# A linear recurrence and a bilinear feed-forward on one core: block 0's up products alone during the weight conversion, and part of block 1 in triples

## The chip, the cores and the metric

One NeuronCore of a Trainium2 chip runs the whole program. The time is device microseconds (us) from the first to the last instruction of an execution, with what lies around them. The kernel before took 598.5 us as the median of three runs (598.17 to 599.41).

The core has five engines that work side by side, each on its own queue in order: PE (matrix products), DVE (element-wise and scans), ACT (activation functions and copies), POOL (element-wise, slower) and SP, which here only issues transfers. An instruction that waits holds everything behind it on its own engine.

## The reference

Two layers in sequence. Layer 1 is a recurrence for each of 4 x 8 heads with a 48 x 48 state; layer 2 is a bilinear feed-forward on 3072 tokens of 384 channels:

```python
f = 1 / (1 + exp(-f_logit))
for t in range(768):
    state = f[:, :, t, :, None] * state + einsum('bhd,bhe->bhde', k[:, :, t], v[:, :, t])
    y[:, :, t] = einsum('bhd,bhde->bhe', q[:, :, t], state)
x = y.transpose(0, 2, 1, 3).reshape(3072, 384)
out = ((x @ w_a) * (x @ w_b)) @ w_out      # w_a, w_b: 384 x 1536, w_out: 1536 x 384
```

`q, k, v, f_logit` arrive as 32-bit floats, the three weight matrices as 64-bit floats.

## The kernel before, in words

**Attention units and blocks.** The 3072 tokens form 8 blocks of 384 (`BLK`). The recurrence of a block is done in two units (four heads each), 16 units in all. Unit 2b and 2b+1 make block b. A unit's *front* (`front_parts`) is: two sigmoids on ACT (one of 1-f with its accumulator), one affine step on POOL, and on DVE scans and the products into `k_in` and `q_in`. Its *core* (`core_parts`) is small matmuls on PE (scores L387, transposes L411, gains L435, within L484, across L510) with a mask on DVE, a copy of the transposes on ACT (`turned`, L420), state additions on DVE, copies out on ACT and stores to `xT`, which is the block's x with channels on the partitions. Scores need `q_in` of their unit.

**The feed-forward of a block.** The d_ff axis has 12 tiles (`ft`) of 128. An *up* (`up_steps`, L593) is one `ft` of one block done directly: three matmuls 128x128 by 128x384 into the bank of b, then three into the bank of a. Each 32-bit matmul of the program is two hardware matmuls in the trace, so an up is 12 of them. Then `product` copies b out of its bank on ACT (the *factor copy*, L613) and multiplies a by it on DVE (L615). There are four banks `ps_f`, handed out in turn, so that up n takes the banks of up n-2: its first half can begin only when the factor copy of up n-2 has been made, its second half only when the product of up n-2 has been taken.

Blocks 2 to 7 do not use ups. They use *triples* (`up_triples`, L715): for j = 0..3, three `ft` at once (j, j+4, j+8) by an algorithm with 15 block products of half width instead of 18. It needs sums of rows of x (`combine_x`, L699) and sums of columns of the weights (`combine_w_ba`), and costs copies on ACT (L1271) and additions on DVE (L707). Products with `w_out` (`down`, L808) take two groups of 128 tokens at a time, by seven products instead of eight, with sums of `w_out` (`combine_w_out`) and of the operands.

**Converting the weights.** The 64-bit weights arrive as 20 pieces (`weight_pieces`): b and a alternate, piece 0 and 1 for ft 0, 2 and 3 for ft 1-2, up to 10 and 11 for ft 9-10, the half-sized 12 and 13 for ft 11; 14 to 19 are `w_out`. The conversion of one (`from_double`) is: on ACT an `Abs` of the high words (L58), an `Identity` of the low words (L59), a `Sign` (L62) and a `Relu` of that (L63), on POOL a minimum (L60) behind the `Abs`, on DVE a shift (L68) behind POOL and an addition into the weights (the *put*, L73, in three rows for pieces 0 to 13). The intermediate buffers `thirds` and `bits` are three deep: the `Abs` of piece i overwrites what the put of piece i-3 reads. Raw pieces land in four places `raws4`; pieces 4 and 5 land in rows 0 and 1 of `groups`.

**The order.** Up to about 66 us of the span the order on every engine is written out by hand: units 0 to 3, pieces 0 to 9, and the ups of block 0 for ft 0 to 5. Then, before the change, the rest of the ups alternate between block 1 and block 0 (`ups`, L1087), so that the weights are needed at half the rate. The first 13 of these are in the written-out part, with conversions between them; the last 5 and all that follows (`main`) are given to a list scheduler. This planner walks through `main`, the sequence of PE products with the copies and sums that free their banks, and places the steps of side lines (`Line`: sums of `w_out`, sums of x, unit cores, unit fronts, loads, sums of `w_ba`) wherever by its own costs (`BEAT` 653 ns for a product of `main`, a load for each step) they delay no step of `main` beyond its due beat. It decides the order on each engine before the kernel runs; on the chip only semaphores hold. `past` and `needs` are a line's conditions, `marks`/`beside` force a line to be done ahead of a point of `main`.

Of the sums of `w_ba` before the change, two- and three-term sums are made by ACT copies (`write`, 6 of them, L628) and accumulating transfers on the POOL queue (`add_by_dma`, 11 of them, L625), and four by DVE additions (L1226).

Of the kernel before, what the change touches and what calls it, by code (L numbers as in the profile page):

```python
# [22 lines left out]
BLK = 384  # L23
# [113 lines left out]
def by_quotients(ctx, tc, q, k, f_logit, v, moe_w_a, moe_w_b, moe_w_out, out, ident, weights, bad):  # L137
# [53 lines left out]
    raw_places = itertools.cycle([raws4[:, PIECE * i:PIECE * i + PIECE] for i in range(4)])  # L191
# [43 lines left out]
    EARLY = (4, 5)  # L235
# [3 lines left out]
    def load_weights(n=1):  # L239
        for _ in range(n):  # L240
# [4 lines left out]
            if src.dtype != FP32:  # L245

                if len(raws) in EARLY:
                    raw = groups[:, EARLY.index(len(raws))].bitcast(mybir.dt.uint64)
                else:
                    raw = next(raw_places)  # L250
                raw = raw[:, 0:k * m].rearrange("p (k m) -> p k m", k=k)
# [18 lines left out]
    def end(n):  # L270

        while ended[0] < min(n, len(todo)):
            begin(ended[0] + 1)
            next(going[ended[0]], None)
            ended[0] += 1
            if ended[0] > 2 and ended[0] - 1 not in EARLY:
                load_weights()

    def convert(n):
        while ended[0] < min(n, len(todo)):  # L280
            end(ended[0] + 1)
            begin(ended[0] + 2)
# [6 lines left out]
    firsts = groups[:, len(EARLY)].rearrange("p (u n s) -> p u n s", u=NQ, n=2)  # L289
# [317 lines left out]
    def product():  # L607

        if not factors:
            return  # L610
        blk, ft, ps = factors.pop(0)
        b_sb = next(b_copies)
        nc.scalar.copy(b_sb, ps["b"][:, 0:BLK])  # L613
# [10 lines left out]
    def add_by_dma(to, x):  # L624
        nc.gpsimd.dma_start(out=to, in_=x, accum_op=ALU.add)  # L625

# [3 lines left out]
    def w_sums(steps, width):  # L630

        for to, x, what in steps:
            if what in (1, -1):
                yield ACT, width, 0, write, to, x, what
            elif what == "+":
                yield POOL, 1300, 0, add_by_dma, to, x
            else:
                yield DVE, width + 200, 0, nc.vector.tensor_tensor, to, x, *what
# [19 lines left out]
    def combine_w_ba():  # L658
# [10 lines left out]
        )  # L669
        return w_sums((  # L670
            (s[1], a12, 1), (s[4], a33, -1), (s[5], a11, -1), (s[1], a22, "+"), (s[4], a31, "+"), (s[5], a31, "+"),
            (s[3], a22, 1), (s[2], a12, 1), (s[0], a21, 1), (s[1], a23, "+"), (s[4], a21, "+"), (s[5], a32, "+"),
            (s[3], a23, "+"), (s[2], a22, "+"), (s[0], a32, "+"), (s[3], a32, "+"), (s[2], a21, "+"),
        ), 1000), w_sums((
            (a31, a11, (a31, ALU.subtract)), (a31, a31, (a33, ALU.add)),
            (a22, s[1], (a31, ALU.subtract)), (a22, a22, (a13, ALU.add)),
# [32 lines left out]
    def up_triples(blk):  # L709
# [28 lines left out]
        for j in range(NJ3):  # L738
# [9 lines left out]
            first, second = (x.rearrange("p (g n t) -> p g n t", g=2, n=2) for x in pairs)  # L748
# [15 lines left out]
            yield copy(3, first[:, :, 1], u)  # L764
# [3 lines left out]
            yield copy(3, first[:, :, 0], v)  # L768
            yield on(DVE, 870, 0, add_steps, c[:, :, 1:3, 1], c[:, :, 1:3, 1], first, copied=True)
# [5 lines left out]
            yield copy(3, second[:, :, 1], v)  # L775
# [5 lines left out]
            yield copy(2 if j == NJ3 - 1 else 3, second[:, :, 0], v)  # L781
            yield times(u, "u5", j)
            yield add(3, 2, 0, u)
            yield on(DVE, 870, 0, add_steps, c[:, :, 0], c[:, :, 0], second, copied=True)
# [153 lines left out]
    with tc.manual_schedule():  # L938
# [98 lines left out]
        end(3)  # L1037
        load_unit(3, "v")
        end(4)
        turn(2)  # L1040
# [21 lines left out]
        load_weights(2)  # L1062
# [6 lines left out]
        end(7)  # L1069
        mask(3)  # L1070
# [5 lines left out]
        end(8)  # L1076
        carried(3)
        product()
        begin(10)
        end(9)  # L1080
        up(0, 5)
# [5 lines left out]
        ups = [(0, 6), (0, 7)]  # L1087
        for i in range(8, NFT):
            ups += [(1, i - 8), (0, i)]
        ups += [(1, i) for i in range(NFT - 8, NFT)]  # L1090
# [532 lines left out]
```

## Time and profile before

| what | value |
|---|---|
| median of 3 runs | 598.5 us |
| profiled execution, its own time | 597.91 us |
| its span, first to last instruction | 596.2 us |
| PE / DVE / ACT / POOL busy | 571.8 / 412.3 / 269.3 / 77.0 us |
| mean granted PE clock | 0.997 |
| hand-written part ends, up of (block 0, ft 6) begins on PE | 66.20 us |
| last up ends on PE | about 138.8 us |

How to read the profile: busy time is by engine; a line such as `L593 PE MATMUL ps_f<-xT,w_ba ... x288 | 95.6, 489 | ...` is a group of instructions of one source line with its count, its busy time in us and the mean of one in ns. A timeline line is start, length, engine, line, operation, and in brackets the engine's idle time before it and who ended it. The chain is the series of waits followed back from the last instruction; where it lies on one engine for long, that engine sets the time there. A window line gives the busy time of every engine in a stretch of the span, then the granted PE clock and the share of the transfer engines.

### The profile page before, as it was taken

The numbers are of one execution on the slowest core, as the hardware profiler recorded it, in microseconds if no ns is written. First come the engines' busy times: TensorE is split into PE (matmuls) and PEld (weight loads), VectorE is DVE, ScalarE is ACT, GpSimd is POOL, SyncE is SP. The second block draws the span as 40 slices with busy tenths as digits, with TensorE's granted clock in tenths as the row PEclk, the third lists the DMA queues.
The fourth block names the chain that finished last, engine by engine and source line by source line (L and its number), as shares of the span: only waits on it lengthen the run. The fifth ranks groups of instructions, "written<-read, shape, count | busy, mean of one in ns | idle before, by whom it ended". The sixth has DMA issues, their size and how long they took to land.

```text
span 596.2 us, 13953 instructions
## 1 busy us (share of the span) xinstructions
PE 571.8 (96%) x5802; PEld 512.0 (86%) x5802; DVE 412.3 (69%) x786; ACT 269.3 (45%) x507; POOL 77.0 (13%) x71
## 2 busy tenths in 40 slices
PE   3899999999999999999999999999999999999995
PEld 1655655567999999999999999999999999999995
DVE  6899445599977778958895677838784256745741
ACT  6589959743123464245521354325431345144300
POOL 6254525354000000000000000000000000000000
PEclk9999999999999999999999999999999999999998
DMA  8697699099542440044004400050001100000000
GB/s 215 184 257 226 211 252 263 0 157 186 118 134 66 113 100 3 17 120 93 2 2 128 117 10 1 2 127 21 3 1 47 48 1 0 2 27 1 0 30 32
DMA packets 33273, 49.43 MB, mean 83 GB/s; under 512 B 3952, under 2 KB 24976, under 8 KB 33200
## 3 DMA queue, kind: packets, MB, share of 16 engines
q1 hardware_dynamic: 30000, 42.38, 26.0%
q0 software_dynamic: 3056, 5.92, 5.8%
q8 instruction: 47, 0.77, 0.6%
q14 instruction: 26, 0.21, 0.1%
q10 hardware_dynamic: 144, 0.15, 0.1%
HBM read 33.23 MB, written 4.72 MB: 64 GB/s over the span
## 4 chain that ended last, share of the span: by engine, by line
PE 84%; DVE 10%; issue 2%; ACT 1%; DMA 1%; SPq 0%; DVEq 0%; ACTq 0%
PE ps_f L715 35%; PE ps_f L808 28%; PE ps_f L593 13%; PE ps_y L484 2%; DVE inv L329 2%; PE ps_y L510 2%; PE ps_x L387 2%; PE ps_x L435 1%; PE ps_x L411 1%; DVE sums L707 1%; DVE groups L707 1%; DVE spare L329 1%; DVE f_in L316 1%; DVE q_in L333 1%; DVE w_ba L73 1%
## 5 line engine op out<-in xcount | busy, mean ns | idle before, releaser
L593 PE MATMUL ps_f<-xT,w_ba 128*128 128x384 f32 x288 | 95.6, 489 | 1.9 <-DMA xT<-y 1.4
L1271 ACT COPY sums<-ps_f 128x384 f32<-128x384 f32 x120 | 57.5, 480 | 75.9 <-PE ps_f L715 68.2
L593 PEld LDWEIGHTS ps_f<-xT,w_ba 128*128 128x128 f32 x288 | 53.9, 190 | 38.6 <-issue 2.6
L1271 ACT COPY groups<-ps_f 128x384 f32<-128x384 f32 x120 | 57.7, 481 | 62.9 <-PE ps_f L715 39.9
L715 PE MATMUL ps_f<-xT,w_ba 128*128 128x192 f32 x384 | 78.4, 327 | 0.0
L715 PEld LDWEIGHTS ps_f<-xT,w_ba 128*128 128x128 f32 x384 | 64.7, 190 | 0.2
L715 PE MATMUL ps_f<-groups,w_ba 128*128 128x192 f32 x288 | 55.5, 328 | 0.0
L715 PE MATMUL ps_f<-x_sums,raw 128*128 128x192 f32 x288 | 54.0, 331 | 1.2 <-DVE groups L707 0.9
L808 PE MATMUL ps_f<-w_out,sums 128*128 128x192 f32 x288 | 52.2, 329 | 0.3 <-DVE groups L615 0.3
L808 PE MATMUL ps_f<-w_out,groups 128*128 128x192 f32 x288 | 51.7, 328 | 0.0
L715 PEld LDWEIGHTS ps_f<-x_sums,raw 128*128 128x128 f32 x288 | 46.9, 190 | 4.3 <-DVE groups L707 1.8
L808 PE MATMUL ps_f<-spare,sums 128*128 128x192 f32 x288 | 49.0, 326 | 0.0
L715 PEld LDWEIGHTS ps_f<-groups,w_ba 128*128 128x128 f32 x288 | 47.8, 190 | 0.5 <-ACT groups L1271 0.3
L808 PEld LDWEIGHTS ps_f<-w_out,sums 128*128 128x128 f32 x288 | 47.1, 190 | 1.3 <-DVE groups L615 0.6
L808 PEld LDWEIGHTS ps_f<-w_out,groups 128*128 128x128 f32 x288 | 47.1, 190 | 0.7
L312 POOL TENSOR_SCALAR inv<-inv 128x768 f32<-128x768 f32 x14 | 13.1, 935 | 267.3 <-ACT inv L309 267.2
L808 PEld LDWEIGHTS ps_f<-spare,sums 128*128 128x128 f32 x288 | 47.1, 190 | 0.1
L60 POOL TENSOR_SCALAR sums<-sums 128x768 f32<-128x768 f32 (+1 forms) x20 | 39.7, 1983 | 45.0 <-ACT sums L58 44.8
L707 DVE TENSOR_TENSOR sums<-sums,groups 128x768 f32<-128x768 f32 x36 | 34.7, 965 | 14.2 <-ACT groups L1271 13.7
L707 DVE TENSOR_TENSOR sums<-ps_f,sums 128x384 f32<-128x384 f32 x60 | 32.9, 553 | 16.5 <-PE ps_f L715 15.0
L715 PE MATMUL ps_f<-x_sums,w_ba 128*128 128x192 f32 x192 | 39.3, 327 | 0.5 <-DVE sums L707 0.5
L715 PE MATMUL ps_f<-xT,raw 128*128 128x192 f32 x192 | 39.4, 328 | 0.0
(136 smaller groups left out, 868.0 us busy)
## 6 DMA issues: line engine op xcount, KB each, us to landing
raw<-w_ba POOLq DMA_DIRECT2D x11, 512.0 KB, 8.5
k_in<-in_k_dram SPq DMA_DIRECT2D x32, 144.0 KB, 3.8
q_in<-in_q_dram SPq DMA_DIRECT2D x32, 144.0 KB, 4.2
v_in<-in_v_dram SPq DMA_DIRECT2D x16, 288.0 KB, 5.4
raw<-in_moe_w_out_dram SPq DMA_DIRECT2D x6, 768.0 KB, 6.3
out_dram<-o SPq DMA_DIRECT2D x24, 192.0 KB, 1.9
f_in<-in_f_logit_dram SPq DMA_DIRECT2D x28, 144.0 KB, 2.9
xT<-y SPq DMA_DIRECT2D x45, 72.0 KB, 2.2
```

Of the source, the lines that this page charges most:

```text
L60: nc.gpsimd.tensor_scalar(h, h, HI_MAX, None, ALU.min)
L73: nc.vector.tensor_tensor(dst[:, rows], hu[:, rows], bit[:, rows], ALU.add)
L312: nc.gpsimd.tensor_scalar(inv, inv, EXP_K, 1.0, ALU.mult, ALU.add)
L329: nc.vector.tensor_tensor_scan(inv[:, w], inv[:, w], none[:, 0:C], first, ALU.mult, ALU.add)
L387: nc.tensor.matmul(ps[h][SUB * p:SUB * p + SUB, o:o + SUB], lhsT=kf[r, tokens(n, c, p)], rhs=qf[r, tokens(n, c, p)], start=True, stop=True,)
L484: nc.tensor.matmul(ps[p][e:e + D, o:o + SUB], lhsT=t["v"][r, n, c, h * D:h * D + D], rhs=at[r, h, o:o + SUB], start=o == 0, stop=True, ski ...
L510: nc.tensor.matmul(ps[p][e:e + D, o:o + SUB], lhsT=st[j][r, n], rhs=qf[r, tokens(n, c, p)], start=False, stop=True, skip_group_check=True,)
L593: nc.tensor.matmul(ps[nm][:, 0:BLK], lhsT=w[:, kt, ft * 128:ft * 128 + 128], rhs=xT[blk][:, kt], start=kt == 0, stop=kt == NKT - 1,)
L707: nc.vector.tensor_tensor(to, x, y, op)
L715: nc.tensor.matmul(ps[:, g], lhsT=sums_of_w[name][:, g, 128 * j:128 * j + 128], rhs=sums_of_x[blk][name], start=start and g == 0, stop=Tru ...
L808: nc.tensor.matmul(to, lhsT=x[:, i // 2, i % 2], rhs=w[:, NI * (i % 2) + i // 2], start=start and i == 0, stop=i == HFT - 1, skip_group_ch ...
L1271: do(*args)
```

## The change

* Block 0's ups for ft 6 to 11 now come one after the other, with no ups of block 1 between them. Block 1 does six ups directly (ft 0, 4, 8 and 1, 5, 9, that is j = 0 and 1), and its other six `ft` in two triples (j = 2 and 3), behind block 0's first pair of `down`.
* Everything from up (0, 6) on is planned by the list scheduler: the conversions of pieces 9 to 19 are now three lines of steps (`piece_steps`), the loads of pieces and of units 4 to 6 are in its load line. `convert` is gone; `beside` marks `("w", ft)` force the pieces of an `ft` ahead of its up.
* The odd pieces above 10 (11, 13, 15, 17, 19) have their sign taken by one DVE instruction (`sign_bits`: a mask of the upper 16 bits) instead of `Sign` and `Relu` on ACT.
* The raw pieces use six places, four in `raws4` and two in `groups`, in the order `PLACES`.
* The factor copy and the product are two steps of `main`, due 3 and 5 beats on.
* The sums of `w_ba` are 13 DVE additions in three lots: `w_early` (4, behind piece 13), `w_late` (4), `w_over` (5, behind the last up). The ACT copies and the 11 accumulating transfers are gone.
* The sums of x are also made for block 1, the first five behind the last up, the rest behind the first `down`.

```diff
+    PLACES = (0, 1, 2, 3, 4, 5, 0, 1, 2, 3, 4, 5, 0, 1, 2, 3, 4, 5, 2, 3)
...
+    def piece_steps(i, sign_on_dve):
...
+        def sign_bits():
+            x = raws[i].bitcast(U16).rearrange("p k (n four) -> p (k n) four", four=4)[:, :, 3]
+            nc.vector.tensor_scalar(upper, x, 0x8000, None, ALU.bitwise_and)
...
+        yield ACT, 150 + n, 0, exponent
+        yield ACT, 240 + n, 0, rounded
+        yield POOL, 350 + 240 * n // 100, 0, bounded
+        if sign_on_dve:
+            yield DVE, 100 + n, 0, sign_bits
+        else:
+            yield ACT, 300 + 220 * n // 100, 0, signs
+        yield DVE, 200 + n // 2, 0, shifted
...
         return w_sums((
-            (s[1], a12, 1), (s[4], a33, -1), (s[5], a11, -1), (s[1], a22, "+"), (s[4], a31, "+"), (s[5], a31, "+"),
-            (s[3], a22, 1), (s[2], a12, 1), (s[0], a21, 1), (s[1], a23, "+"), (s[4], a21, "+"), (s[5], a32, "+"),
-            (s[3], a23, "+"), (s[2], a22, "+"), (s[0], a32, "+"), (s[3], a32, "+"), (s[2], a21, "+"),
+            (s[1], a22, (a23, add)), (s[2], a12, (a22, add)), (s[2], s[2], (a21, add)), (s[0], a21, (a32, add)),
         ), 1000), w_sums((
-            (a31, a11, (a31, ALU.subtract)), (a31, a31, (a33, ALU.add)),
-            (a22, s[1], (a31, ALU.subtract)), (a22, a22, (a13, ALU.add)),
+            (s[3], s[1], (a32, add)), (s[1], s[1], (a12, add)), (s[4], a33, (a31, less)), (s[4], a21, (s[4], less)),
+        ), 1000), w_sums((
+            (a31, a11, (a31, less)), (s[5], a32, (a31, less)), (a31, a31, (a33, add)),
+            (a22, s[1], (a31, less)), (a22, a22, (a13, add)),
         ), 950)
...
-        ups = [(0, 6), (0, 7)]
-        for i in range(8, NFT):
-            ups += [(1, i - 8), (0, i)]
-        ups += [(1, i) for i in range(NFT - 8, NFT)]
-        alone = len(todo) - 7
-        for n, (blk, i) in enumerate(ups[0:alone]):
-            convert(needed(i))
-            up(blk, i)
-            end(8 + n)
-            product()
-            begin(ended[0] + 2)
...
+        DIRECT = 2
+        ups = [(0, i) for i in range(6, NFT)] + [(1, j + NJ3 * k) for j in range(DIRECT) for k in range(NI)]
...
+        for blk, i in ups:
+            if not blk:
+                beside[len(main)] = "w", i
             main.extend(up_steps(blk, i))
-            main.append(on(DVE, 480, 2, product))
+            main.append(on(ACT, 480, 3, copy_factor))
+            main.append(on(DVE, 480, 5, multiply, copied=True))
...
-            if blk >= 2:
+            if blk:
                 beside[len(main)] = "x", blk
-                main.extend(up_triples(blk))
+                main.extend(up_triples(blk, DIRECT if blk == 1 else 0))
...
+            landed = ()
+            if i >= n_loaded:
+                last_there = max(j for j in range(i) if PLACES[j] == PLACES[i])
+                there = (read[last_there],) if last_there in read else ()
+                landed = (loads.extend([(SP, ISSUE, -3200, load_weights)], there),)
+            convert(i, landed)
...
+                    if beside[done][0] == "w":
+                        now = max(now, line.ends[-1] + LATENCY)
```

## The prediction

> **What bounds the kernel now.** I read the page's busy times first, then PE's waits, then windows by stage, then the chain. PE is the bound nearly from the start. From the page, the chain's shares by engine:
>
> ```profile
> PE 84%; DVE 10%; issue 2%; ACT 1%; DMA 1%; SPq 0%; DVEq 0%; ACTq 0%
> ```
>
> PE's waits after 50 us, all of them (engine, tile, line, releaser; us in total):
>
> ```profile
> PE ps_f L715 <- DVE groups L707: 0.9, 1, 0.9
> PE ps_x L435 <- issue: 0.8, 1, 0.8
> PE ps_f L593 <- DVE w_ba L73: 0.5, 1, 0.5
> PE ps_f L715 <- DVE sums L707: 0.5, 1, 0.5
> PE ps_f L808 <- DVE groups L615: 0.3, 1, 0.3
> PE ps_f L715 <- ACT groups L1271: 0.2, 1, 0.2
> ```
>
> That is 3.2 us in 546. The windows of the stage that the change rewrites (PE, PEld, DVE, ACT, POOL busy):
>
> ```profile
> 66.20:128.00 61.80, 61.80 (x198) 36.45 (x193) 33.40 (x63) 48.43 (x69) 25.43 (x15) 1.00 0.65 164
> 128.00:141.00 13.00, 12.84 (x140) 8.43 (x138) 11.83 (x26) 3.60 (x7) 6.98 (x6) 1.00 0.99 166
> ```
>
> PE has no gap there; ACT is 78% busy. So a PE product saved is time saved, and a PE wait made is time lost, one for one; and a stage in which ACT already works 48 of 62 us is the place to look for new waits.
>
> **What PE saves.** Chain pieces give the price of one hardware matmul: the 192 of the ups from 66.27 took 62.13 us, 0.3236 each (an up: 12 x 0.3236 = 3.88), and 240 of a triple stage took 39.24 us, 0.1635 each.
>
> ```profile
> 66.27 62.13 PE ps_f L593 x192
> 470.16 39.24 PE ps_f L715 x240
> ```
>
> Six ups go: 72 x 0.3236 = 23.3 us. Two triples come: 2 x 15 products x 4 = 120 x 0.1635 = 19.6. **PE saves 3.7 us.** The waits of before between 66 and 150 us (0.3, 0.75, 0.16 = 1.2) go too, since I count the new ones whole.
>
> **What it costs: ACT's queue.** Twelve ups now follow each other: 46.6 us, where 18 took 70. On every engine the order up to the copies of unit 3 and the factor copy of ft 5 is unchanged, so I start from the same moment: PE begins ft 6 at 66.20, ACT makes the factor copy of ft 5 at 67.84 and is free at 68.3. Start to start, a full piece costs ACT 0.80 + 0.90 + 0.94 + 0.94 = 3.58, as here:
>
> ```profile
> 68.81 0.92 ACT L58 ACTIVATE sums<-raw 128x768 f32<-128x768 f32 x1
> 69.61 1.01 ACT L59 ACTIVATE spare<-raw,whole 128x768 f32<-128x768 uint32 x1
> 70.50 0.93 ACT L62 ACTIVATE spare<-raw 128x768 bf16<-128x768 f32 x1
> 71.46 1.08 ACT L63 ACTIVATE spare<-spare 128x768 uint16<-128x768 bf16 x1
> 72.41 0.87 ACT L58 ACTIVATE sums<-raw 128x768 f32<-128x768 f32 x1
> ```
>
> With the sign on DVE it is 1.70; the half piece 12 costs 2.1, 13 costs 1.0; a factor copy 0.40; unit 4's sigmoids 1.06 + 0.75. Added up in the new queue's order, with the buffers' conditions:
> - Piece 10's and 11's Abs and Identity (3.4) and 12's Abs lie ahead of the copy of ft 6 (72.2). Then piece 10's signs, unit 4's sigmoids, the rest of 12, and 13: the copy of **ft 7 comes at 78.9**, done 79.4. PE wants that bank for ft 9 at 77.8: waits **1.6**.
> - Piece 14's Abs overwrites what the last row of piece 11's put reads, and that row stands on DVE behind the product of ft 7: ACT idles to 80.4. Pieces 14 and 15 follow, the copy of ft 8 at 83.8: PE waits **1.0**.
> - In the same way the copies of ft 9, 10, 11 come at 87.8, 92.6 and 98.2 (the last behind piece 19's landing, about 5 us after its place is read; the 768 KB loads here took a median 6.3): PE waits **0.1, 0.9, 1.2**, and **0.8** for two products late on DVE.
> Whatever the waits, ACT has 28.7 us of such work between 68.3 and the copy of ft 11, and PE would need that bank at 93.4: 97.0 + 0.5 - 93.4 leaves 4.1 lost by this queue alone, against 5.6 by the list.
>
> **DVE's queue.** The scores of unit 4 stand in the middle of the twelfth up, and wait for `q_in`. Behind the signs of piece 10 (74.6) DVE's queue up to that product holds: nine shifts 4.9 (0.59, half pieces 0.39), puts 8.8 (1.02, 0.69, w_out 0.90), five sign masks 4.1, eight `w_ba` sums 9.1 (1.14 start to start, row below), four `w_out` sums 5.5 (1.38), nine products 4.2, unit 4's scans and products 6.0. Sum 42.7. With 1.9 of waits for ACT it ends at 119.3. PE comes there at 66.2 + 11.5 x 3.88 + 5.6 = 116.4: waits **2.9**. Without any earlier wait the two would be 117.3 and 110.8, 6.5 apart, so delay taken earlier is partly the same delay.
>
> ```profile
> 157.67 1.22 DVE L1226 TENSOR_TENSOR w_ba<-w_ba 128x1024 f32<-128x1024 f32 x1
> 70.90 0.55 DVE L68 TENSOR_SCALAR sums<-sums 128x768 uint32<-128x768 uint32 x1
> 128.73 0.95 DVE L333 TENSOR_TENSOR q_in<-q_in,f_in 128x768 f32<-128x768 f32 x1
> ```
>
> The mask is not in the trace: a strided 16-bit read of 768. Bounds: 0.55 (the shift above, same count) and 0.96 (768 elements, two inputs); I take 0.9, nearer the upper because its step is four elements. At 0.55 the sum is 1.6 less and PE's waits 0.9 less.
>
> **The end of the ups.** The first `down` takes the bank of the last up, whose factor copy stands on ACT behind the copy of unit 4's transposes: 0.75 + 0.70 + 0.47 from their start, of which the transposes themselves fill 0.65 on PE. PE waits **1.4** with the semaphores. Then 13.7 us of `down` cover five `w_over` sums (5.7) and the sums of x; v1's operand is ready some 3 us early. PE's waits from 66 to 150: 1.6 + 1.0 + 0.1 + 0.9 + 1.2 + 0.8 + 2.9 + 1.4 = **9.9 us**.
>
> **DVE beside POOL.** POOL's ten minima now fall in a stretch in which DVE is full. The trace has both cases: 1.60 instead of 0.95 when a minimum began beside the DVE product, and no loss at 98.59.
>
> ```profile
> 34.21 2.12 POOL L60 TENSOR_SCALAR sums<-sums 128x768 f32<-128x768 f32 x1 [2.40 <-ACT sums L58]
> 34.24 1.60 DVE L333 TENSOR_TENSOR q_in<-q_in,f_in 128x768 f32<-128x768 f32 x1
> ...
> 97.10 2.13 POOL L60 TENSOR_SCALAR sums<-sums 128x768 f32<-128x768 f32 x1 [1.74 <-ACT sums L58]
> ...
> 98.59 0.96 DVE L73 CUSTOM_DVE_ANT_0 w_out<-sums,spare 128x1536 uint16<-128x1536 uint16 x1
> ```
>
> So 0 to 0.65 for each of ten, 0 to 6.5; in this stage's own rows (90 to 110 us) it is 0, and I take 0.5 in all. [...]
>
> **PE's clock.** The clock is 1.00 in each window, and after the longest wait before a matmul, 1.39 us at 33.73, a matmul still took 0.34. The new waits reach 2.9. [...]
>
> **Other edits.** The eleven accumulating transfers and six ACT copies went on in time that PE covered: nothing gained. Loads come at the same time or earlier. Behind 150 us, DVE has two triples' sums (2 x 6.0: five PSUM sums 0.55, two of 0.96, one of 1.36) and x sums (4) more, less three `w_ba` sums, while it was 81% busy between 141 and 230; there PE already waited 1.9 in all. From 0 to 3 more; I take 0.5.
>
> **The sum**, against the profiled execution's own time of 597.9 (span 596.2 and 1.7 around it): 597.9 - 3.7 - 1.2 + 9.9 + 0.5 + 0.5 = 603.9. The median shown is 0.6 above that execution; between the two readings I say **604.0 us**, 0.9% slower.
>
> **Rivals.**
> 1. *Conversion keeps pace; faster.* Mechanism: ACT's and DVE's queues run shorter than added up, so that factor copies and `q_in` are in time. For it: ACT idled 13 and DVE 28 of 62 us there before. Against: 28.7 us of ACT work stand ahead of a copy wanted 25.1 after ACT is free. It decides where PE's waits fall below 4.9; with waits of 2 in place of 9.9, 597.9 - 4.9 + 2 + 0.5 = 595.5.
> 2. *DVE is the bound beyond this stage.* POOL costs 0.4 a piece (midway between the bounds; ten: 4, of which some 2.5 reach PE) or the triples of block 1 find their sums late (3 us): 606.5.
> 3. *Both of these at once:* 3 and 3 on top of 603.9: 610. Against: the rows of this very stage show no loss beside POOL.
>
> **Chances.** Forecast (waits of 7.5 to 12) 0.57, own range 601.5 to 606; rival 2 0.23; rival 3 0.08; rival 1 0.08; the middle, waits of 4 to 6 (597.3 to 599.7), 0.04. A measurement tells 0.2% (1.2 us) from no change. Slower 0.88, same 0.04, faster 0.08. The range leaves out rival 1 and the far end of rival 3: 599.5 to 608.
>
> **What would show it.** In the profile after: PE's waits in 66 to 125 us, on ACT `x_sums` (factor copies) ahead of ft 9 to (1, 4), and on DVE `q_in` ahead of scores, near 10 us in all; L593 at 216 hardware matmuls instead of 288; no L625 transfers; ACT's idle time between 68 and 98 under 2 us and DVE's between 80 and 119 under 1. Wrong would be: PE without gaps there, the sign mask far from 0.9, or waits grown behind 150.

## The result, and the profile after

The kernel after takes **607.8 us** (median of 5 executions, 606.0 to 608.1), the kernel before 598.2 on the same chip: a ratio of 1.0148, 95% interval 1.0135 to 1.016. It is 9.6 us slower. The profiled execution after has a time of 607.9 and a span of 606.2.

From the page of the kernel after: busy times, the granted clock in 40 slices, the chain's shares, and the group of the ups.

```profile
PE 573.2 (95%) x5850; PEld 518.2 (85%) x5850; DVE 439.5 (72%) x821; ACT 261.9 (43%) x506; POOL 65.6 (11%) x60
...
PEclk9999999989999999999999999999999999999999
...
PE 74%; DVE 12%; DMA 5%; issue 3%; ACT 3%; SPq 1%; DVEq 0%; ACTq 0%
...
L635 PE MATMUL ps_f<-xT,w_ba 128*128 128x384 f32 x216 | 75.8, 503 | 7.1 <-ACT x_sums L656 3.8
```

The ups fell from 288 to 216 hardware matmuls, as the diff says, and yet PE is busy 1.4 us longer. PE's share of the chain fell from 84 to 74%, and that of DVE, transfers and ACT grew. One slice, the ninth, has a clock digit under 9. PE's waits between 66.8 and 150 us (tile, line, releaser: us in total, times, longest):

```profile
PE ps_f L635 <- ACT x_sums L656: 3.8, 4, 1.3
PE ps_x L429 <- DVE q_in L375: 2.3, 1, 2.3
PE ps_f L846 <- ACT x_sums L656: 1.3, 1, 1.3
PE ps_f L635 <- DVE groups L661: 1.2, 1, 1.2
```

That is 8.5 us (added before rounding) where the kernel before had 1.0. The windows of the stage (PE, PEld, DVE, ACT, POOL busy, then the clock), the two shown of before and two of 3.4 us around the scores of unit 4:

```profile
66.20:128.00 61.80, 53.04 (x247) 29.61 (x243) 51.98 (x79) 36.59 (x55) 23.25 (x13) 0.97 0.49 143
128.00:141.00 13.00, 13.00 (x123) 12.72 (x124) 12.14 (x20) 0.96 (x3) 0.00 (x0) 1.00 0.01 1
118.80:122.20 3.40, 1.10 (x49) 1.04 (x50) 2.72 (x6) 1.87 (x3) 0.83 (x1) 1.00 0.00 0
122.20:125.60 3.40, 3.40 (x6) 1.82 (x7) 3.40 (x4) 0.00 (x0) 0.00 (x1) 0.50 0.00 0
```

PE had no gap in the first window before; now 8.8 of 61.8 us are empty, and DVE is busy for 52.0 in place of 33.4. The last line was not forecast: in the 3.4 us behind the scores PE ran at half clock. PE's timeline shows where (start, us, and in brackets the idle time ahead):

```profile
80.03 4.14 PE L635 MATMUL ps_f<-xT,w_ba 128*128 128x384 f32 x12 [1.29 <-ACT x_sums L656]
...
97.95 2.20 PE L635 MATMUL ps_f<-xT,w_ba 128*128 128x384 f32 x6 [1.16 <-DVE groups L661]
...
121.10 1.03 PE L429 MATMUL ps_x<-q_in,k_in 48*64 48x64 f32 x48 [2.32 <-DVE q_in L375]
122.05 3.90 PE L635 MATMUL ps_f<-xT,w_ba 128*128 128x384 f32 x6
...
127.88 1.57 PE L846 MATMUL ps_f<-w_out,groups 128*128 128x192 f32 x8 [1.27 <-ACT x_sums L656]
```

Six matmuls of the same shape take 2.20 us at 97.95 and 3.90 at 122.05. ACT's timeline around two of the late copies:

```profile
79.52 0.46 ACT L656 COPY x_sums<-ps_f 128x384 f32<-128x384 f32 x1
80.93 0.93 ACT L296 ACTIVATE sums<-raw 128x768 f32<-128x768 f32 x1 [0.95 <-DVE w_ba L316]
...
96.62 0.89 ACT L296 ACTIVATE sums<-raw 128x768 f32<-128x768 f32 x1 [1.17 <-DVE w_out L316]
...
100.18 0.83 ACT L656 COPY x_sums<-ps_f 128x384 f32<-128x384 f32 x2
```

Conversion steps that stand ahead of a factor copy on ACT (L656) wait for DVE, and the copy waits with them.

### The profile page after: what moved, and what is told of

Its sections match the earlier page's. It is cut to its first block, busy times and chain, and to the rows that moved or that the text cites. A ratio compares the mean times of both kernels' runs of the same rounds, so it can differ in the third digit from the quotient of the medians.

```text
span 606.2 us, 14061 instructions
## 1 busy us (share of the span) xinstructions
PE 573.2 (95%) x5850; PEld 518.2 (85%) x5850; DVE 439.5 (72%) x821; ACT 261.9 (43%) x506; POOL 65.6 (11%) x60
## 4 chain that ended last, share of the span: by engine, by line
PE 74%; DVE 12%; DMA 5%; issue 3%; ACT 3%; SPq 1%; DVEq 0%; ACTq 0%
PE ps_f L753 40%; PE ps_f L846 26%; DMA raw<-in_moe_w_b_dram 3%; PE ps_y L526 2%; PE ps_x L429 2%; DVE raw L1306 1%; PE ps_x L453 1%; PE ps_y L552 1%; DVE groups L745 1%; PE ps_x L477 1%; DVE inv L371 1%; PE ps_f L635 1%; DVE sums L313 1%; DVE q_in L375 1%; DVE sums L745 1%
## 5 line engine op out<-in xcount | busy, mean ns | idle before, releaser
L1352 ACT COPY sums<-ps_f 128x384 f32<-128x384 f32 x130 | 62.3, 481 | 82.0 <-PE ps_f L753 72.5
L1352 ACT COPY groups<-ps_f 128x384 f32<-128x384 f32 x130 | 62.6, 481 | 71.0 <-PE ps_f L753 46.3
L753 PE MATMUL ps_f<-xT,w_ba 128*128 128x192 f32 x416 | 85.2, 328 | 0.0
L635 PE MATMUL ps_f<-xT,w_ba 128*128 128x384 f32 x216 | 75.8, 503 | 7.1 <-ACT x_sums L656 3.8
L635 PEld LDWEIGHTS ps_f<-xT,w_ba 128*128 128x128 f32 x216 | 40.3, 193 | 38.4 <-ACT x_sums L656 6.7
L753 PEld LDWEIGHTS ps_f<-xT,w_ba 128*128 128x128 f32 x416 | 70.1, 190 | 0.8 <-ACT groups L1352 0.5
L753 PE MATMUL ps_f<-x_sums,raw 128*128 128x192 f32 x312 | 58.4, 331 | 1.8 <-DVE groups L745 1.0
L753 PE MATMUL ps_f<-groups,w_ba 128*128 128x192 f32 x312 | 59.9, 328 | 0.0
L753 PEld LDWEIGHTS ps_f<-x_sums,raw 128*128 128x128 f32 x312 | 51.0, 190 | 5.0 <-DVE groups L745 2.7
L753 PEld LDWEIGHTS ps_f<-groups,w_ba 128*128 128x128 f32 x312 | 51.7, 190 | 0.6 <-ACT groups L1352 0.2
L745 DVE TENSOR_TENSOR groups<-ps_f,groups 128x384 f32<-128x384 f32 x65 | 34.7, 549 | 6.9 <-PE ps_f L753 6.6
```

Source lines behind the costliest of these rows:

```text
L635: nc.tensor.matmul(ps[nm][:, 0:BLK], lhsT=w[:, kt, ft * 128:ft * 128 + 128], rhs=xT[blk][:, kt], start=kt == 0, stop=kt == NKT - 1,)
L745: nc.vector.tensor_tensor(to, x, y, op)
L753: nc.tensor.matmul(ps[:, g], lhsT=sums_of_w[name][:, g, 128 * j:128 * j + 128], rhs=sums_of_x[blk][name], start=start and g == 0, stop=Tru ...
L1352: do(*args)
```

## The experiments

All are edits of the kernel after; the fillers of the first and fifth run add matmuls that nobody reads. Each time is a median; behind it stand the ratio to the kernel before, taken on the same chip, and its 95% interval. The rows are those of one profiled execution of each. "Half clock" is a granted PE clock of 0.50. Theory 1, the prediction's, says that PE waits because ACT's and DVE's queues hold more than the shorter stage covers. The rival, theory 2: the list scheduler puts steps in an order that suits neither, because it takes the engines for freer than they are. A third question is what made the half clock.

### A filler in the gap (first and fifth run)

```diff
         ps = pair_of(home(u))
+        if u == 2 * NQ:
+            for _ in range(8):          # 4 in the fifth run
+                nc.tensor.matmul(ps[0][:, 0:BLK], lhsT=ident, rhs=xT[0][:, 0], start=True, stop=True)
```

> Eight matmuls of 128x128 by 384 columns that nobody reads are put ahead of unit 4's scores (8 x 0.32 = 2.6 us), where PE waited 2.32 us for q_in and where the clock record then stood at 0.5 for 3.41 us. Theory A (the idle gap, followed by 1 us of small score matmuls, halves the clock): the wait for q_in falls below 0.4 us, no stretch of 0.5 follows, and the six-matmul up behind the scores takes 2.0 us in place of 3.9: 1.9 us less, less 0.3 for the surplus of the filler, so 606.2 against 607.8. Theory B (the half clock is something of its own, a start-up or power effect): the 0.5 stretch stays where it is and the time is 607.8 to 608.3.

> The filler of the first run, halved: four independent matmuls (eight on the hardware, 8 x 0.32 = 2.6 us) ahead of unit 4's scores; the eight of the first run were sixteen on the hardware, took 5.3 us and so made the scores 2.7 us later than the wait had. Theory A (the gap before the scores halves the clock): no stretch at 0.5, the six matmuls behind the scores take 2.2 us in place of 3.9, the scores begin at most 0.6 us later: 606.0 to 606.8 against 607.8. Theory B (the surplus work of the first run, not the filled gap, kept the clock up): a gap or a half clock stays and the time is 607.5 or more.

Eight matmuls took 5.3 us, twice what was expected, and the time was 608.8 us (ratio 1.018, 1.0162 to 1.0197). Counted from the start of ft 6, the scores came 2.75 us later than in the kernel after, but the first triple only 0.96 later: 1.8 came back. Four matmuls gave 606.0 us (1.0131, 1.0109 to 1.0153). PE's timeline of the fifth run:

```profile
118.02 2.74 PE L427 MATMUL ps_x<-xT,ident 128*128 128x384 f32 x8
120.69 0.93 PE L432 MATMUL ps_x<-q_in,k_in 48*64 48x64 f32 x48
121.55 2.20 PE L638 MATMUL ps_f<-xT,w_ba 128*128 128x384 f32 x6
```

In this stage neither run has the gap or the half clock, and the six matmuls are back at 2.20 us. The gap, 2.32 us in the kernel after, made the half clock there. Its price is 1.8 us: in the fifth run the scores begin 54.3 us behind the start of ft 6, as in the kernel after, and the first triple 73.9 instead of 75.7. The intervals of the ratios overlap, so the times alone wouldn't show it; the rows do.

### The late sums let go later (second run)

```diff
-        for_ba.extend(w_late, pieces())
+        for_ba.extend(w_late, pieces(), past=behind["direct"] - 12)
```

> The four sums of w_ba that stand on DVE ahead of unit 4's k and q products (w_late, 4 x 1.14 = 4.6 us) are let go only when twelve steps of the ups are left. Theory A (PE's wait for q_in is the length of DVE's queue, so shortening it takes the wait and the half clock away): wait for q_in under 0.5 us, no 0.5 stretch, copy waits ahead of ft 9 to (1, 4) as they were (3.8 to 5 us together); 2.3 + 1.9 less, 603.6 against 607.8. Theory B (DVE is the bound of the whole stage up to the triples, so the delay only comes back): the sums now end under the first down, PE waits 2 to 4 us more at v1 or at the first copies behind it, and the time is 605.5 to 608.

606.8 us (1.0147, 1.0124 to 1.017). Theory A fell; the time lies in theory B's range, but PE waits at none of the places that B named. The scheduler saw room and moved unit 4's scores from the twelfth up into the eleventh, where the same wait and the same half clock met them, as PE's timeline shows:

```profile
115.92 1.54 PE L429 MATMUL ps_x<-q_in,k_in 48*64 48x64 f32 x48 [2.36 <-DVE q_in L375]
117.39 3.29 PE L635 MATMUL ps_f<-xT,w_ba 128*128 128x384 f32 x6
```

This fits a wait that is the difference between when the scheduler believes `q_in` ready and when it is: a shorter queue moves both. The scheduler's own estimate is in no trace.

### All signs on DVE (third run)

```diff
-            steps = list(piece_steps(i, i > 10 and i % 2))
+            steps = list(piece_steps(i, i >= 10))
```

> All weight pieces from 10 on take their sign as one DVE mask; ACT loses the two steps of pieces 10, 12, 14, 16 and 18 (4 x 1.88 + 1.0 = 8.5 us), DVE gains five masks (5 x 0.6 = 2.9 us). Theory A (factor copies come late because conversion steps stand ahead of them on ACT): PE's waits on x_sums ahead of ft 9 to (1, 4) fall from 3.8 us to under 1; the wait for q_in grows by what DVE gained, to 4 to 6 us (a half-clock stretch behind it stays); 605.5 to 607.5 against 607.8. Theory B (ACT is late because it waits for DVE's rows and the landing of the pieces, not for its own work): the waits on x_sums stay over 2.5 us and the time grows with DVE's work, to 609 to 611.

609.95 us (1.0195, 1.0177 to 1.0214), as theory B had it. ACT was relieved (24.8 us busy from 66 to 110 us, where it was 32.8), but PE waited 3.3 us for a factor copy, 3.0 for a stretch that the profile ends with a transfer, 2.6 for `q_in`, and the clock was halved twice in this stage. ACT's timeline of this run says why less work did not help:

```profile
88.31 0.93 ACT L296 ACTIVATE sums<-groups 128x768 f32<-128x768 f32 x1 [2.43 <-DVE w_out L316]
...
96.47 0.90 ACT L296 ACTIVATE sums<-raw 128x768 f32<-128x768 f32 x1 [2.67 <-DMA raw<-in_moe_w_out_dram]
```

A conversion step waits for the buffer that DVE's put of an earlier piece still reads, or for its piece to land, and the factor copies queued behind it on ACT wait too. What makes the copies late is the waiting steps ahead of them, not ACT's sum of work.

### Block 1 between block 0 again (fourth run)

```diff
-        ups = [(0, i) for i in range(6, NFT)] + [(1, j + NJ3 * k) for j in range(DIRECT) for k in range(NI)]
+        ups = [(0, 6), (0, 7), (0, 8), (1, 0), (0, 9), (1, 4), (0, 10), (1, 1), (0, 11), (1, 5), (1, 8), (1, 9)]
```

with pieces 16 and 17 in places 0 and 1, and `w_early` behind piece 17.

> The same twelve ups and the same triples, but the six ups of block 1 are put between those of block 0: ft 6, 7, 8, (1, 0), ft 9, (1, 4), ft 10, (1, 1), ft 11, (1, 5), (1, 8), (1, 9). Pieces 16 and 17 land in the places of 12 and 13, and the first four sums of w_ba wait for piece 17. Theory A (block 0 alone makes each factor copy and piece due too soon, DVE's queue stays as long): waits on x_sums and on groups fall from 5 us to under 2; DVE still ends its queue at about 119, so the wait for q_in grows to 4 to 6.5 us; 605 to 608. Theory B (the order alone makes all waits): copy waits and the wait for q_in both vanish and the time is 598 to 600.5. Theory C (the order is of no effect, since ACT's sum of work decides): the waits on x_sums stay at 3 us or more and the time is 607 to 609.

608.0 us (605.9 to 609.3; 1.0173, 1.0149 to 1.0198). Waits on `x_sums` and `groups` in the ups fell from 4.9 to 2.6 us, so the order of blocks matters there; but PE then stood 2.6 us at the first `down` for a product on DVE and, behind 150 us, 6.0 in place of 1.9, where unit 4 came only in the first triple (its scores at 136.7 us); that this made the later waits is argued, not tested. The sum is what theory A said (upper end), the place of the new wait is not. The rows are those of the fastest of the four executions: it took 605.9 us at a mean clock of 0.997 and shows no half clock, the other three 607.1 to 609.3 at 0.990 to 0.992.

### All of block 1 direct (seventh run)

```diff
-        DIRECT = 2
+        DIRECT = NJ3
```

with no triples and no sums of x for block 1; block 2's sums of x are let go where block 1's were.

> Block 1's up products all direct (18 ups in place of 12 and two triples); block 0 is still alone while weights are converted. Theory A (the triples save PE 3.7 us as counted, and the cost lies in the ups of block 0): PE's waits on x_sums and groups between 66 and 105 us stay at 5 us, PE has 72 hardware matmuls of 0.3236 more and 120 of 0.1635 less; the later down takes the DVE wait away (2.3 + 1.9): 607 to 609.5 against 607.8, well over 598. Theory B (the triples' sums and their early deadline make the cost): the time falls to 603 or less. Theory C (both, and the stage's end keeps its wait): 610 to 612.

608.6 us (1.0163, 1.0142 to 1.0184). PE's waits between 60 and 200 us:

```profile
PE ps_f L635 <- ACT x_sums L656: 3.6, 4, 1.2
PE ps_x L429 <- DVE q_in L375: 2.3, 1, 2.3
PE ps_f L635 <- DVE groups L661: 1.2, 1, 1.2
PE ps_f L846 <- ACT x_sums L656: 0.5, 1, 0.5
```

To 121 us these are the waits of the kernel after, with the half clock behind them. They come with block 0's ups, and not with the triples of block 1. Theory A's range holds; the wait for `q_in`, which it let vanish, stayed. The triples' gain is there in the rows: from ft 6 to PE's last matmul, less the waits listed, the profiled execution has 526.1 us, that of the kernel after 522.2. The medians show only 0.8 of it. Here the profiled execution (610.1 us, mean clock 0.992) isn't a typical one: two of the four took 607.8 and 607.7 at 0.998.

### The late sums on POOL (eighth run)

```diff
-            yield DVE, width + 200, 0, nc.vector.tensor_tensor, to, x, *what
+            if pool:
+                yield POOL, 3000, 0, nc.gpsimd.tensor_tensor, to, x, *what
+            else:
+                yield DVE, width + 200, 0, nc.vector.tensor_tensor, to, x, *what
```

with `pool` true for `w_late`.

> The four sums of w_late go from DVE (1.14 us each) to POOL, which is idle there from 100 us on; the program's costs take 3.0 us for one. DVE's queue is 4.6 us shorter, and unit 4's scores are put one or two ups earlier. Theory A (DVE's length is what PE waits for at the end of the stage): wait for q_in under 1 us, no half clock, 603.5 to 605.5. Theory B (the scores are put too early by the scheduler wherever DVE ends, as in the second run): a wait of 2 to 2.5 us and a half clock stay, 606 to 608. Theory C (POOL and DVE disturb each other): DVE's sums beside POOL's take 1.5 us and more in place of 1.2, or v1 waits for POOL's sums; over 608.

616.2 us (1.03, 1.0274 to 1.0325): theory C, and stronger. The timelines of POOL (first line) and of DVE:

```profile
99.35 5.50 POOL L1309 TENSOR_TENSOR raw<-raw,w_ba 128x1024 f32<-128x1024 f32 x2
...
99.61 3.11 DVE L358 TENSOR_TENSOR_SCAN f_in<-f_in,zero 128x384 f32<-128x384 f32 x1
102.76 2.11 DVE L361 TENSOR_TENSOR held<-f_in,least 128x2 f32<-128x2 f32 x1
```

The scan takes 0.95 us elsewhere in this run, the second one 0.16 in the third run: they lost 2.16 and 1.95 us beside POOL sums of 2.75. PE then waited 4.3 us for one product, and 3.1 for `q_in`.

### The scheduler told of the backlog (sixth run)

The scheduler's `now` is the moment at which PE begins ft 6 (66.9 us), and it took every engine for free. In the trace of the kernel after ACT is free at 69.0 and DVE at 69.6.

```diff
-        now, free_at, done, arrived = 0, [0] * 5, 0, 0
+        now, free_at, done, arrived = 0, [0, 2200, 2100, 0, 0], 0, 0
```

> The list scheduler's clock starts with ACT 2.1 us and DVE 2.2 us busy, as the trace shows them when PE begins ft 6 (ACT is free at 69.0, DVE at 69.6, PE starts at 66.9), where it took all engines for free. Nothing but the order changes: factor copies of ft 7 to 11 come one conversion step earlier on ACT, unit 4's scores move from the twelfth up into the first triple. Theory A (the waits are made by the order: conversion steps are put ahead of copies because the scheduler takes ACT and DVE for freer than they are): waits on x_sums fall from 5.1 us to under 1.5, the wait for q_in and the half clock go; 600.5 to 603.5 against 607.8. Theory B (the sum of work on ACT and DVE decides): the waits change their names, to groups and w_ba from DVE ahead of the ups, the first down or v1, and keep 7 us or more; 606 to 608.

611.9 us (1.023, 1.021 to 1.025), and neither theory as written. In the stage theory A held: waits from 66 to 150 us of 2.6 in place of 8.5, no half clock there, the first triple at 130.9 us in place of 142.5, though with 2.2 us of unit 4's PE work (scores, transposes, gains) still to come. All of it and more was lost later (10.7 us of waits behind 150 us), most of it in one wait with 6.8 us of half clock behind it, here in the timelines of PE and of DVE:

```profile
262.03 1.65 PE L753 MATMUL ps_f<-x_sums,raw 128*128 128x192 f32 x4 [5.67 <-DVE x_sums L737]
...
261.02 0.56 DVE L737 TENSOR_TENSOR x_sums<-xT 128x384 f32<-128x384 f32 x1 [3.73 <-DMA out_dram<-o]
```

Block 3's sums of x waited for rows of its second unit, whose last products ran on PE at 250 to 252 us (the profile names another transfer of that time as the releaser). With the stage's sums still on DVE, the units had slipped behind the feed-forward that needs them.

### Unit 4 ahead of the sums (tenth run)

The sixth run's edit, and the unfinished steps of unit 4's `core` and `fore` lines tried ahead of the other lines in `in_order`.

```diff
-            return [loads, *sorted(left, key=lambda x: of_piece[x][len(x.ends)]), *lines[1 + len(conversions):]]
+            return [loads, *sorted(left, key=lambda x: of_piece[x][len(x.ends)]), *([core] if len(core.ends) < n_core4 else []), *([fore] if len(fore.ends) < n_fore4 else []), *lines[1 + len(conversions):]]
```

> The scheduler's clock starts with ACT and DVE busy as in the sixth run, and unit 4's own steps go ahead of the w_out and w_ba sums, so that its scores stand in the ninth up and not in the first triple. Theory A (the sixth run lost behind 150 us only because unit 4 came late): the stage keeps its 2.5 us of copy waits, the 5.7-us wait for block 2's sums of x goes to under 1.5; 601 to 604. Theory B (DVE is full up to the first triple, and whatever is put ahead makes the rest late): the sums now wait, 4 us or more are lost at the first down and v1, with or without a half clock; 605 to 609.

614.6 us (1.0271, 1.0252 to 1.0289): theory B, and worse. PE waited 2.5 us for a factor copy at 92 us, with a half clock behind it. The sums moved behind unit 4 came so late that the sums of x reached DVE only when PE was already waiting for v1, the first product of the first triple (timeline of PE, then DVE):

```profile
135.69 0.91 PE L753 MATMUL ps_f<-x_sums,raw 128*128 128x192 f32 x4 [2.12 <-issue]
...
134.65 0.55 DVE L737 TENSOR_TENSOR x_sums<-xT 128x384 f32<-128x384 f32 x1
```

and the wait for rows at 259 us stayed, at 5.9 us (it is block 3's; the expectations call it block 2's). DVE is busy for 62.9 of the 71 us from 66 us to the first triple: an order that puts one thing ahead makes another late.

### The first eight sums of w_ba off DVE (ninth run), and both (eleventh run)

```diff
-            (s[1], a22, (a23, add)), (s[2], a12, (a22, add)), (s[2], s[2], (a21, add)), (s[0], a21, (a32, add)),
+            (s[1], a22, 1), (s[2], a12, 1), (s[0], a21, 1), (s[1], a23, "+"), (s[2], a22, "+"), (s[0], a32, "+"), (s[2], a21, "+"),
...
-            (s[3], s[1], (a32, add)), (s[1], s[1], (a12, add)), (s[4], a33, (a31, less)), (s[4], a21, (s[4], less)),
+            (s[4], a33, -1), (s[4], a31, "+"), (s[3], s[1], 1), (s[3], a32, "+"), (s[1], a12, "+"), (s[4], a21, "+"),
```

where 1 and -1 are an ACT copy and "+" an accumulating transfer on POOL's queue, as before the change. The eleventh run adds the sixth run's edit.

> The first eight sums of w_ba are made as before the change, by five copies on ACT (1.05 us each) and eight accumulating transfers, in place of eight sums on DVE (1.14 each). DVE's queue in the stage is 9.1 us shorter; the scheduler now puts unit 4's scores into the eighth up. Theory A (DVE is too full, and this part of the change made it so): the wait for q_in and the half clock go, copy waits ahead of ft 9 to (1, 4) stay at 3.5 to 5 us; 602 to 604.5 against 607.8. Theory B (the scheduler's order makes the waits, whatever DVE holds): the wait for q_in stays at 2 us or more at its earlier place, with more waits behind it in unit 4's chain; 605 to 608.

> Both causes at once: the scheduler's clock starts with ACT 2.1 and DVE 2.2 us busy, and the first eight sums of w_ba go by copies on ACT and accumulating transfers. Unit 4's scores stand in the twelfth up. Theory A (order on ACT and DVE's fullness are the two causes, and nothing else is lost): waits from 66 to 150 us fall from 8.6 to 2.5 to 4, no half clock; 606.2 - 5.5 - 1.9 + 1.7 around the span = 600.5, 598.5 to 601.5 in all. Theory B (transfers late or ACT's copies in the way): v1 or the first down waits 3 us or more; over 602.

Alone it gives 607.4 us (1.016, 1.014 to 1.018): theory B. With DVE shorter the scheduler put unit 4's scores ahead of the seventh up (72 matmuls of the ups come before them in the trace; the expectation has the eighth), and there `q_in` was 6.9 us late:

```profile
100.11 1.66 PE L429 MATMUL ps_x<-q_in,k_in 48*64 48x64 f32 x48 [6.91 <-DVE q_in L375]
```

With copy waits of 2.7 that is 9.6 us in the stage, and the clock at half for 6.8 us; the time is level with the kernel after's. Both edits give 602.05 us (1.0063, 1.0041 to 1.0085), near theory A's upper end and at theory B's lower one. Copy waits are 1.9 us, and one wait of 2.4 with a half clock is left, ahead of the first `down`'s second part. The timelines of PE, DVE and POOL around it:

```profile
123.52 3.90 PE L854 MATMUL ps_f<-w_out,sums 128*128 128x192 f32 x12 [2.44 <-DVE groups L661]
...
120.53 0.42 DVE L371 TENSOR_TENSOR_SCAN inv<-inv,zero 128x128 f32<-128x128 f32 x1 [4.15 <-POOL inv L354]
...
118.39 1.20 POOL L674 DMA_DIRECT2D raw<-w_ba  x1 [3.84 <-DMA raw<-w_ba]
119.67 0.82 POOL L354 TENSOR_SCALAR inv<-inv 128x768 f32<-128x768 f32 x1
```

Unit 5's step stood on POOL behind the transfers, its scan on DVE behind that, and the last up's product on DVE behind the scan.

### Unit 5 held back (twelfth run)

```diff
                 ready = fore.extend(
-                    [(e, load, 0, *do) for part in front_parts(s) for e, load, *do in part], loaded[s]
+                    [(e, load, 0, *do) for part in front_parts(s) for e, load, *do in part], loaded[s],
+                    past=behind["direct"] if s == 2 * NQ + 1 else 0,
                 )
```

on top of the eleventh.

> The eleventh run, with unit 5's own steps held back until the direct ups are done. In the eleventh run DVE stood 4.15 us at unit 5's scan, which waits for POOL's step on unit 5, and that step stands on POOL behind the accumulating transfers; the product of the last up stood behind the scan, PE waited 2.4 us for it ahead of the second part of the first down and ran at half clock for 3.4 us. Theory A (that was all that is left of the loss in the stage): neither the wait nor the half clock; 602.05 - 2.4 - 1.9 = 597.8, 597 to 599, level with before. Theory B (the work is only late again elsewhere): unit 5's chain starves block 2's triples, PE waits 3 us or more behind 150 us; over 600.5.

**597.5 us** (11 executions, 596.2 to 598.8), against 598.25 for the kernel before: a ratio of 0.9988, 0.9979 to 0.9998. The whole loss is gone, as theory A had it. PE's waits from 60 to 150 us, then those behind 150 us:

```profile
PE ps_f L635 <- ACT x_sums L656: 2.0, 3, 0.9
PE ps_f L761 <- ACT sums L1361: 0.3, 1, 0.3
...
PE ps_f L761 <- DVE groups L753: 1.8, 2, 1.0
```

4.1 us in all, where the kernel after has 10.4, and the clock's record has no stretch at half until PE has ended. Unit 5 held back was not run without the other two edits.

## Why the prediction was right, and where it was off

Direction and stated range held: 604.0 was forecast, with 599.5 to 608, and it is 607.8. The increase is 9.6 us where 5.5 was said. That the range held is partly luck: 607.8 lies outside the 601.5 to 606 given to the forecast's own mechanism, and 0.2 us inside an upper end that rivals 2 and 3 had set. What filled the distance was none of theirs but, for the largest part, a half clock for which nothing had been put into the sum. Of the signs named, the 216 matmuls and DVE's idle time (0.6 us between 80 and 119) held; PE's waits are 7.3 us to 125 us and 8.5 to 150 (near 10 said), ACT idles 3.1 us between 68 and 98 (under 2 said), and the sign mask at 0.60 is one of the signs of being wrong. Step by step:

**What PE saves.** The counts are as said (216 hardware matmuls of the ups). With the stage mended, in the twelfth run, PE's time from ft 6 to its last matmul, less the waits listed, is 518.1 us against 521.1 before: 3.0 of the 3.7. The waits of before that go are 1.0 us and not 1.2: the prediction's 0.16 is in part the 0.3 counted beside it.

**ACT's queue.** PE began ft 6 at 66.86 in place of 66.20. To within this later start the list held for the copies of ft 7, 8 and 9, which came at 79.5, 84.4 and 88.3 (said: 78.9, 83.8, 87.8). Those of ft 10 and 11 came at 94.1 and 100.2 (92.6, 98.2), 0.8 and 1.3 later than the start explains. PE's waits there were 1.29, 0.71, 1.24, 0.53 and 1.16 for a product: 4.9 in place of 5.6. What failed is a reading of them. "This queue alone" was given 28.7 us of ACT work and 4.1 of loss; the third run took 8 us of that work away and lost more, and the sixth cut the waits to 2.4 by order alone. Not the amount was at fault but which steps stand ahead of the copies, and what those wait for.

**DVE's queue.** `q_in` was ready at 121.0, said 119.3; PE came there at 118.8, said 116.4, and waited 2.32, said 2.9. The wait is near because both sides slipped. Of DVE's terms the sign mask was too high (it takes 0.60; the lower bound was 0.55, I took 0.9; five of them 1.3 less) and the loss beside POOL too low, next. As with ACT, the length of the queue is not the wait: shortened by 4.6 or 9.1 us, it left waits of 2.4 and 6.9 (second and ninth run), for the scores were moved up with it. The step that I left out is that the scheduler's place for the scores follows its own estimate.

**The end of the ups.** 1.4 was said; 1.27.

**DVE beside POOL.** 0.5 was taken out of bounds of 0 and 6.5; the rows of the stage show eight DVE steps lengthened by 0.24 to 0.67, together 4.5 us. Four of them, with two of POOL's minima, a put that lost nothing, and a mask with nothing on POOL beside it:

```profile
76.82 1.20 DVE L313 TENSOR_SCALAR sums<-sums 128x768 uint32<-128x768 uint32 x1
...
82.09 0.98 DVE L313 TENSOR_SCALAR sums<-sums 128x384 uint32<-128x384 uint32 x1
...
91.58 2.13 POOL L302 TENSOR_SCALAR sums<-sums 128x768 f32<-128x768 f32 x1 [1.65 <-ACT sums L296]
91.60 1.63 DVE L316 CUSTOM_DVE_ANT_0 w_out<-sums,spare 128x1536 uint16<-128x1536 uint16 x1
...
94.25 2.12 POOL L302 TENSOR_SCALAR sums<-sums 128x768 f32<-128x768 f32 x1 [0.54 <-ACT sums L296]
94.28 1.21 DVE L313 TENSOR_SCALAR sums<-sums 128x768 uint32<-128x768 uint32 x1
95.62 0.96 DVE L316 CUSTOM_DVE_ANT_0 w_out<-sums,spare 128x1536 uint16<-128x1536 uint16 x1
...
104.35 0.60 DVE L310 TENSOR_SCALAR spare<-raw 128x768 uint16<-128x768 uint16 x1
```

Rival 2 had taken 4 us for this, which is near; how much of it reached PE isn't shown. The low value rested on a put at 98.59 that lost nothing, and on rows of the same stage. Here too most steps beside a minimum lose nothing (the puts at 89.19 and 95.62 take 0.96). What tells them apart in this trace is the moment: seven of the eight began 0.01 to 0.26 us behind the start of a POOL step, like the product at 34.24 that the prediction shows, while the put at 98.59 began 1.49 behind. In the kernel before, between 69 and 111 us, the only DVE steps that began within 0.7 us behind a minimum's start were seven products of the ups (L615, with a bank `ps_f` as an input); they began 0.26 to 0.63 behind it and took 0.56, as elsewhere. So those rows do not show what a shift, a put or a mask loses there; the kernel after, with DVE busy for 52.0 us of the first window in place of 33.4, has seven steps of these three kinds that meet a start. It is not a strict rule: in the third run a mask that began 0.87 us behind a start took 1.16. Beside POOL's sums with two inputs more was lost: in the eighth run a scan of 0.95 took 3.11.

**PE's clock.** This step failed outright: with waits of up to 2.9 us the sum has no term for the clock, and the longest wait that it had to go by was 1.39 us. That longer ones would cost no more than their length was the author's estimate; the runs showed otherwise. A wait of 2.32 us, with 1 us of small score matmuls behind it, halved the clock and cost 1.8 us, shown by the fifth run. It is the largest part of what the forecast was short of. The last section has what the rows say of the other waits.

**Behind 150 us.** 0.5 was taken; PE's waits there are 1.9 us where they were 1.6, so about 0.4 more (the prediction's 1.9 for the kernel before takes in the 0.3 at 141 us).

**The sum.** Against the forecast 603.9, the profiled 607.9 has 1.8 for the clock, 0.7 for the later start, 0.4 more behind PE's last matmul, and 0.2 for the waits of before; the new waits are 1.4 less (8.5 for 9.9), those behind 150 us 0.1 less. The later start need not be the change's doing: in the kernel after and the twelve runs, which share the order up to there, ft 6 begins between 65.5 and 67.1 us. Further, each wait costs 0.23 us more than its listing: a stretch that ends in a wait shows the last matmul's own run-out as busy (36 matmuls of 0.3236 are 11.65, and 11.88 were listed ahead of the wait at 78.7). The kernel after has five such stretches more, 1.2 us. Another 0.9 is in pauses inside groups listed as one (54 matmuls in 18.09 us, 24 in 8.47). These come to 3.7 of the 4.0; 0.5 of the sum had been kept for POOL, whose loss, where it reaches PE, lies in the waits, so 0.8 stays without a name. The PE saving, 3.0 in the twelfth run where 3.7 was taken, may be most of that.

**Rivals.** Rival 1 (conversion keeps pace, 595.5) is what the kernel comes near to with another order and eight sums taken off DVE: the twelfth run is at 597.5, with 2.0 us of copy waits. It also shows how little was to be had: 3.7 us of PE work counted bought 0.7 us of time. Rival 2's second half (the triples of block 1 find their sums late, 3 us) did not come: PE's waits behind 150 us grew by 0.4.

## What to carry to other kernels

When a stage is shortened on the bound engine, the other engines' work in it does not shrink; add up their queues to the moment at which the bound engine wants each result, and do it in the order that the scheduler writes, with the steps ahead of it that wait. A list scheduler that starts with engines taken for free, or that trusts its own estimate of a result, puts a wait wherever its estimate is early: shortening the late engine's work moves the wait, and what removed it here was the true backlog at the start, work taken off the full engine, and one unit held back, together; of these, the first two alone gave +4.1 and -0.4 us against the kernel after, and the third was not run alone.

## What the runs showed of the hardware that was not expected

**Half clock came and went in steps of 3.413 us.** In the traces' clock records every stretch, half or full, begins and ends at multiples of 3.413 us from the record's first entry, up to the record's end. The kernel after has 105.813 us at full clock, 3.413 at half and 477.866 at full, which are 31, 1 and 140 steps to within 0.05 us; the kernel before has 576.852 at full, 169 steps. Each step taken as a window and laid over PE's waits, in the kernels before and after and the twelve runs, for windows that are themselves at full clock (the grid is placed to some 0.2 us, so the counts at the edges are too):

| idle time of PE within one window | cases | clock in the next window |
|---|---|---|
| behind 30 us: 1.2 to 1.95 us | 28 | 1.00 in all |
| behind 30 us: 2.00 to 2.72 us | 10 | 0.50 in all |
| behind 30 us: 3.41 us (whole window) | 3 | 0.50 in all |
| at 20 to 25 us: 1.70 to 1.89 us | 6 | 0.50 in all |

The kernel after has both outcomes: 1.29 us idle in the window from 77.85 us and a clock of 1.00 in the next, 2.29 idle in the one from 118.81 and 0.50 in the next. So in these runs the half clock went with how much of a wait fell into one window, and not with the wait's length. Nor did 2 us divide all cases. The last row is from the attention units at the start, where PE runs only small matmuls (48 of 48x64 in 0.9 us, and the like) between its waits: 1.70 us idle was followed by half clock there, 1.60 (ninth run) was not. In four of these six runs the clock then stayed at half through a whole window of such matmuls with 0.1 to 0.3 us idle. Why less idle time went with half clock there was not tested. PE's timeline of the third run has a wait of 3.04 us split over two windows as 1.23 and 1.81, and full speed behind it; that of the fourth has one of 2.63 split as 1.58 and 1.05, and 12 matmuls in 2.22 us behind it, where the eleventh run, with 2.44 in a single window, took 3.90:

```profile
98.67 6.07 PE L635 MATMUL ps_f<-xT,w_ba 128*128 128x384 f32 x18 [3.04 <-DMA k_in<-in_k_dram]
```

```profile
120.21 2.22 PE L846 MATMUL ps_f<-w_out,sums 128*128 128x192 f32 x12 [2.63 <-DVE groups L661]
```

Behind 30 us, then, idle time of 2.00 us or more inside one window was followed by a window at half clock in each of the 13 cases here. What that costs beyond the wait is shown for one of them, the wait of 2.32 us of the kernel after: 1.8 us (fifth run).

**DVE lost about 2 us beside POOL's sums, 0 to 0.67 beside its minima.** In the kernel after, beside POOL's one-input steps, the minima of 2.1 to 2.8 us above all, a DVE step lost 0 to 0.67 us, and it was mostly the step that began just behind the minimum's start; in the eighth run, beside a sum of 2.75 us with two inputs, a scan of 0.95 took 3.11 and a step of 0.16 took 2.11.
